# Lightning attention and a low-rank mixer: the masked quarter of the scores left out from step twelve, with the keys of every second pair of heads turned

## The chip, the cores and the metric

The kernel runs on one core of a Trainium2 chip. The metric is the time on the device of one execution, in microseconds (us), as the median of several runs. Before the change it is 673.5 us (three runs, 673.49 to 673.6).

## What is computed

Two blocks, one after the other, in float32. The first is linear attention with a decay per head, for 4 batches, 8 heads, 768 rows and 64 elements a head:

```python
Dmask = np.where(rel >= 0, lam ** rel, 0.0)            # rel = query row - key row
intra = einsum('bhic,bhjc->bhij', qb, kb) * Dmask      # scores, masked
intra = einsum('bhij,bhjd->bhid', intra, vb)
inter = einsum('bhid,bhde->bhie', qb * lam_pow, kv_state)
out   = intra + inter
kv_state = lam_block * kv_state + einsum('bhsd,bhse->bhde', kb * rev_pow, vb)
```

What matters here: a score counts only where the query row is not before the key row. In a tile of 128 keys by 128 queries, the quarter with the keys 64 to 127 and the queries 0 to 63 is zero after the mask. (The reference works in blocks of 64 rows, the kernel in tiles of 128; the result is the same.)

The second block mixes along the sequence with rank 32, `u = x + (U V)-mix of x`, and ends with `u + max(u @ w_ch1, 0) @ w_ch2`, where w_ch1 is 512 x 2048. These two products are most of the time.

## The kernel before, in words

The attention stage takes 24 steps, `s = 0..23`: a step is one tile of 128 rows of one batch, all 8 heads (6 tiles a batch, so step 12 is the first of the third batch). Heads go in four pairs, `a = 0..3`, with `x = 0, 1` inside a pair. Each step has these pieces; the order on every engine is the order in which the program is written, as the stage is put under a manual schedule (the list `pieces`, lines 553 to 574):

- `prep(s+1)`: q and k of the next step are transposed on TensorE (L348, banks pq and pk), and ScalarE copies them to qt and kt (L351).
- `scale(s+1)`: GpSimd multiplies qt by powers of the decay (qs, L376) and the k of the step after (ks, L365).
- `mix(s-7)` (pu L506 on TensorE, x_nat L509 on VectorE), and at the first step of a batch also `low` (pp L461) and `low_rows` (p_h L481, later the low part L487 on VectorE; ScalarE copies h, h2 and l2, L492, L493, L496, which the next `mix` reads). pp lies in the bank tag of pq.
- `intra(s)`: masked scores times v (px L446), after which ScalarE copies px to x_nat (L451).
- `state(s)`: the new state of keys and values (pkv L411, in the bank tag of pk; kv L417 or L419 on VectorE). Left out in a batch's last step.
- `turned`: ScalarE's u_hl (L542) and GpSimd's u_d (L543) for an earlier tile.
- `scores(s+1)` (pss L393), `inter(s+1)` (px L434), `masked(s+1)` (L402, VectorE), `fade(s+1)` (faded L385, ScalarE).
- `turn(s-7)`: the mixed tile is transposed (put L523), VectorE takes its high and low parts (ut L528, u_hl L539).
- Between them pieces of the preparation of the weights (`aside` and `late`: sc, m, wf, w on VectorE and ScalarE, L154 to L217).

One matmul in float32 is two records in the trace. Scores are written with the keys on the partitions of pss and the queries along its columns. In steps 0 to 11 a score matmul covers 128 keys; from step 12 on it is cut in two halves of 64 keys, so that each matmul uses a quarter of the array (`x` chooses the rows, the half of the keys the columns). sm, the masked scores, is one buffer; pss is one buffer of two banks, x in the first and the second.

From 121 us on come the two large products (`hidden`, L722 and L732, and `product`, L855 to L859).

Of the kernel before, what the change touches and what calls it, by code (L numbers as in the profile page):

```python
# [8 lines left out]
FP32 = mybir.dt.float32  # L9
# [3 lines left out]
ALU = mybir.AluOpType  # L13

P = 128
# [3 lines left out]
def kernel(  # L19
# [28 lines left out]
    nc = tc.nc  # L48

    B, H, S, D = q.shape  # L50
    HP = H // 2
    NT = S // P
# [45 lines left out]
    def tmp(name):  # L98
        return wconv.tile([P, C], FP32, tag="tmp", bufs=3, name=name)
# [139 lines left out]
    att = att_ctx.enter_context(tc.tile_pool(name="att", bufs=1))  # L239
# [5 lines left out]
    def two_banks(name, tag):  # L245
        return psf.tile([P, 2, N], FP32, tag=tag, name=name)
# [12 lines left out]
    raw = {}  # L259
# [30 lines left out]
    mask = consts.tile([P, 2, HP, P], FP32, name="mask")  # L290
# [33 lines left out]

    xs = {}
    st = {}
    kv = {}
    half = [slice(0, D), slice(D, P)]  # L330
# [55 lines left out]

    def scores(s):
        qt, kt = st[s]["qt"], st[s]["kt"]
        st[s]["pss"] = pss = two_banks("pss", "pss").rearrange("p x (a i) -> p x a i", a=HP)
        for a in range(HP):  # L390
            for x in range(2):
                for rows in half if s >= 2 * NT else [slice(0, P)]:
                    nc.tensor.matmul(  # L393
                        out=pss[rows, x, a, :], lhsT=kt[half[x], a, rows],
                        rhs=qt[half[x], a, :], start=True, stop=True,
                    )

    def masked(s):
        pss = st[s].pop("pss")
        st[s]["sm"] = sm = att.tile([P, 2, HP, P], FP32, tag="sm", bufs=1, name="sm")  # L400
        for x in range(2):
            nc.vector.tensor_tensor(out=sm[:, x], in0=pss[:, x], in1=mask[:, x], op=ALU.mult)  # L402

    def state(s):
        c = s % NT
# [33 lines left out]
    def intra(s):  # L439
        first = s % NT == 0  # L440
        sm, vr, px = st[s]["sm"], raw[s, "v"], st[s]["px"]
        px = px[:, :, 0 : HP * D].rearrange("p x (a e) -> p x a e", a=HP)
        for a in range(HP):
            for x in range(2):
                for t in range(2):
                    nc.tensor.matmul(  # L446
                        out=px[half[t], x, a, :], lhsT=sm[:, x, a, half[t]],
                        rhs=vr[:, 2 * a + x, :], start=(first and a == 0), stop=(a == HP - 1),
                    )
        xs[s] = x_pool.tile([P, C], FP32, tag="x", name="x_nat")  # L450
        nc.scalar.copy(xs[s].rearrange("p (a x e) -> p x a e", a=HP, x=2), px)  # L451


    pps = {}
# [56 lines left out]
    uhl, ud, turned = {}, {}, {}  # L511
# [42 lines left out]
    for s in range(NS):  # L554
        b, c = divmod(s, NT)
        done = s - NT - 1
        more = s + 1 < NS
        step = [("prep", s + 1), ("scale", s + 1)] * more
        step += [("late", s - 1)] * (s == NT)
        step += [("mix", done)] * (0 <= done < NS - NT - 1)  # L560
        step += [("low", b - 1)] * (c == 0 and b > 0)
        step += [("low_rows", b - 1)] * (c == 0 and b > 0)
        step += [("intra", s)]
        step += [("next_of_low", b - 1)] * (c == 0 and b > 0)
        step += [("late", s)] * (s < NT - 1 or s == NT) + [("state", s)]
        step += [("next_of_low", b - 1)] * (c == 0 and b > 0)
        step += [("turned", done - 1)] * (done > 0) + [("late", s)] * (done >= 0)
        step += [("next_of_low", b - 1)] * (c == 0 and b > 0)
        step += [("scores", s + 1)] * more
        step += [("aside", s)] * (s >= 2 * NT)  # L570
        step += [("inter", s + 1), ("masked", s + 1), ("fade", s + 1)] * more
        step += [("aside", s)] * (s < 2 * NT)
        step += [("turn", done)] * (done >= 0 and done // TG < FG)
        pieces += step
    waiting = {name: list(range(NS)) for name in "qkv"}

    def load_next(name, engine=nc.sync):
# [3 lines left out]

    run = {
        "prep": prep, "fade": fade, "scores": scores, "masked": masked, "inter": inter,
        "intra": intra, "state": state,
        "low": low, "low_rows": low_rows, "next_of_low": next_of_low, "mix": mix, "turn": turn,
        "scale": scale, "turned": lambda s: turned.pop(s)(),
    }
    def v_steps():

# [186 lines left out]
    c0, b = NS - NT, B - 1  # L776
# [181 lines left out]
```

## Time and profile before

| | |
|---|---|
| time, median of 3 | 673.5 us |
| span of the profiled execution | 672.5 us |
| attention stage | 0 to about 121 us, 24 steps |
| TensorE busy, 60 to 80, 80 to 100, 100 to 120 us | 19.54, 19.93, 19.68 of 20 us |
| VectorE busy in the same stretches | 19.51, 18.49, 18.44 |
| ScalarE busy in the same stretches | 13.51, 12.40, 14.23 |
| GpSimd busy in the same stretches | 12.56, 13.23, 14.61 |
| granted TensorE clock | 1.00 throughout |

Busy time of TensorE is from modelled ends of pipelined matmuls, so that a busy engine isn't yet one at its peak; the distance from the start of one group to that of the next tells what a group holds of the engine. An idle engine matters only where another waits for it. The view that tells this is the chain that ended last: the last instruction, what released it, what released that, and so on back to the start. For each piece it gives the start, the length and the engine, tile and line. Where the name of the engine changes, TensorE waited.

### The profile page before, as it was taken

Reading aid. Unit: us, or ns where it says so; the run is one execution under the profiler, and the core shown is the slowest. Engines: PE = TensorE matmul, PEld = TensorE weight load, DVE = VectorE, ACT = ScalarE, POOL = GpSimd, SP = SyncE. Lnnn points to the kernel's source line nnn. Section 1 sums busy time; section 2 is a strip of 40 time slices with the busy share of each in tenths; the row PEclk is TensorE's granted clock in tenths of the full one; section 3 lists DMA queues with packets and bytes.
Section 4 is the critical chain, followed back from the end, with each engine's and each line's share of the span. In section 5 each row is a group of like instructions: output and inputs, shape, how many; then the busy total and the mean of one; then the engine's idle time right before and its main releaser. Section 6 shows DMA issues by size and latency. Waiting matters only on the chain.

```text
span 672.5 us, 13170 instructions
## 1 busy us (share of the span) xinstructions
PE 665.9 (99%) x5124; PEld 545.4 (81%) x5124; DVE 496.6 (74%) x873; ACT 278.7 (41%) x517; POOL 112.8 (17%) x92
## 2 busy tenths in 40 slices
PE   9999999999999999999999999999999999999997
PEld 8888898787888888888888888888888888888885
DVE  4679999777999777777797255786586775865854
ACT  4675767454555444444455121332232322322320
POOL 4455667340000000000000000030030200300300
PEclk9999999999999999999999999999999999999999
DMA  9999993264776555555587999854363363443421
GB/s 208 214 228 239 237 232 109 84 215 156 235 276 240 204 203 204 204 203 204 203 280 253 325 314 387 291 185 140 94 206 107 110 204 94 158 155 95 161 89 62
DMA packets 131775, 131.27 MB, mean 195 GB/s; under 512 B 81346, under 2 KB 89794, under 8 KB 131714
## 3 DMA queue, kind: packets, MB, share of 16 engines
q1 hardware_dynamic: 130656, 130.18, 61.3%
q8 instruction: 40, 0.66, 0.4%
q10 hardware_dynamic: 1058, 0.26, 0.2%
q14 instruction: 21, 0.17, 0.1%
HBM read 80.09 MB, written 50.33 MB: 194 GB/s over the span
## 4 chain that ended last, share of the span: by engine, by line
PE 96%; DVE 2%; ACT 2%; issue 0%; DVEq 0%; ACTq 0%
PE pz L722 27%; PE pz L857 13%; PE pd L732 13%; PE pz L855 13%; PE pd L859 13%; PE pss L393 3%; PE px L446 3%; PE put L523 2%; PE pq L348 2%; PE px L434 1%; PE pkv L411 1%; PE pk L348 1%; PE pp L461 1%; PE pu L506 1%; PE idle L336 0%; ACT qt L351 0%
## 5 line engine op out<-in xcount | busy, mean ns | idle before, releaser
L722 PE MATMUL pz<-u_hl,w 128*128 128x512 f32 x768 | 190.4, 397 | 0.0
L722 PEld LDWEIGHTS pz<-u_hl,w 128*128 128x128 f32 x768 | 144.0, 188 | 35.5 <-issue 0.4
L857 PE MATMUL pz<-w_hl,m 128*128 128x512 f32 x384 | 151.1, 396 | 0.0
L855 PE MATMUL pz<-w_hl,m 128*128 128x512 f32 x384 | 150.9, 396 | 0.0
L859 PE MATMUL pd<-w_d,m 128*128 128x512 f32 x384 | 149.5, 396 | 0.0
L838 ACT ACTIVATE m<-mt 128x512 fp32r<-128x512 f32 x96 | 60.7, 633 | 196.0 <-PE pd L859 141.7
L839 DVE SCALAR_TENSOR_TENSOR m<-rm,m 128x512 fp32r<-128x512 f32 x96 | 71.4, 745 | 52.2 <-ACT m L838 52.1
L884 POOL TENSOR_TENSOR o<-o,u 128x512 f32<-128x512 f32 x20 | 29.9, 1529 | 447.3 <-DVE o L880 447.3
L737 DVE SCALAR_TENSOR_TENSOR r<-pd,r 128x512 f32<-128x512 f32 x96 | 61.8, 685 | 54.0 <-ACT r L728 43.5
L732 PE MATMUL pd<-u_d,w 128*128 128x512 f32 x384 | 98.6, 397 | 0.0
L728 ACT ACTIVATE r<-pz 128x512 f32<-128x512 f32 x96 | 52.2, 596 | 93.6 <-PE pz L722 92.9
L857 PEld LDWEIGHTS pz<-w_hl,m 128*128 128x128 f32 x384 | 72.3, 188 | 17.7
L855 PEld LDWEIGHTS pz<-w_hl,m 128*128 128x128 f32 x384 | 72.3, 188 | 17.6
L859 PEld LDWEIGHTS pd<-w_d,m 128*128 128x128 f32 x384 | 72.3, 188 | 17.6
L732 PEld LDWEIGHTS pd<-u_d,w 128*128 128x128 f32 x384 | 72.1, 188 | 17.3
L840 DVE SCALAR_TENSOR_TENSOR m<-m 128x512 fp32r<-128x512 f32 x96 | 69.0, 720 | 0.9
L837 DVE TENSOR_SCALAR mt<-rm 128x512 uint32<-128x512 uint32 x96 | 46.1, 481 | 28.0 <-DMA rm<-r_d 27.6
L402 DVE TENSOR_TENSOR sm<-pss,mask 128x512 f32<-128x512 f32 x48 | 30.8, 683 | 7.4 <-PE pss L393 7.3
L205 ACT CAST w<-wt 128x512 fp32r<-128x512 f32 x32 | 19.9, 622 | 30.5 <-DVE wt L202 23.4
L376 POOL TENSOR_TENSOR qs<-qt,powq 128x512 f32<-128x512 f32 x20 | 25.9, 1296 | 23.3 <-ACT qt L351 22.3
L446 PEld LDWEIGHTS px<-vraw,sm 128*64 128x64 f32 x768 | 24.7, 137 | 6.0 <-issue 2.4
L446 PE MATMUL px<-vraw,sm 128*64 128x64 f32 x768 | 28.3, 226 | 0.5 <-DVE sm L402 0.4
(88 smaller groups left out, 682.7 us busy)
## 6 DMA issues: line engine op xcount, KB each, us to landing
r_d<-r SPq DMA_DIRECT2D x96, 256.0 KB, 2.5
rm<-r_d SPq DMA_DIRECT2D x96, 256.0 KB, 2.7
words<-in_moe_w_ch_dram SPq DMA_DIRECT2D x30, 512.0 KB, 4.4
w_d<-w SPq DMA_DIRECT2D x16, 768.0 KB, 3.3
w_hl<-w_d SPq DMA_DIRECT2D x16, 512.0 KB, 6.2
vraw<-in_v_dram SPq DMA_DIRECT2D x24, 256.0 KB, 4.6
u_d<-x_nat SPq DMA_DIRECT2D x24, 256.0 KB, 3.5
u<-u_d SPq DMA_DIRECT2D x24, 256.0 KB, 4.1
```

Source lines behind the costliest of these rows:

```text
L446: nc.tensor.matmul(out=px[half[t], x, a, :], lhsT=sm[:, x, a, half[t]], rhs=vr[:, 2 * a + x, :], start=(first and a == 0), stop=(a == HP - 1),
L722: nc.tensor.matmul(out=acc[g][0], lhsT=w[:, n, ct, :], rhs=uhl[g][:, n, ct, :], start=(ct == 0 and n == 0), stop=(ct == CT - 1 and n == 1),)
L728: nc.scalar.mul(rs[g], acc[g][0], 4096.0 + 1.0)
L732: nc.tensor.matmul(out=acc[g][1], lhsT=w[:, 2, ct, :], rhs=ud[g][:, ct, :], start=(ct == 0), stop=(ct == CT - 1),)
L737: nc.vector.scalar_tensor_tensor(rs[g], acc[g][1], 4096.0, rs[g], ALU.mult, ALU.add)
L837: nc.vector.tensor_scalar(t.bitcast(U32), r.bitcast(U32), HI, None, ALU.bitwise_and)
L838: nc.scalar.activation(out=m[:, 0], in_=t, func=AF.Relu)
L839: nc.vector.scalar_tensor_tensor(m[:, 1], r, 0.0, hi, ALU.max, ALU.subtract)
L840: nc.vector.scalar_tensor_tensor(m[:, 2], hi, E, low, ALU.mult, ALU.subtract)
L855: nc.tensor.matmul(out=pz, lhsT=m[:, 0, cols], rhs=hl[:, 0], start=first, stop=False)
L857: nc.tensor.matmul(out=pz, lhsT=m[:, 1, cols], rhs=hl[:, 1], start=False, stop=end)
L859: nc.tensor.matmul(out=pd, lhsT=m[:, 2, cols], rhs=dd, start=first, stop=end)
```

## The change

From step 12 on (`TURNED = 2 * NT`), the matmul for the second half of the keys streams only the 64 queries that it can have a score with; the masked quarter isn't computed. In pairs a = 1 and 3 the halves of the keys are exchanged: keys 64 to 127 go to partitions 0 to 63 of pss and keys 0 to 63 to the others. So each quarter of the array gets two matmuls of 128 columns and two of 64 in a step. In the quarter that isn't written, pss still holds finite numbers of step 11, which the mask sets to zero; for this, pss becomes one tile that is allocated once.

The exchange has to be followed by whatever meets those scores: the mask of the odd pairs is turned by ScalarE over a scratch tile, in three copies in steps 9, 10 and 11 (`turn_mask`), and v of the odd heads' pairs is turned for each step by two ScalarE copies of 64 x 256 into vs (`turn_v`), which stand in ScalarE's queue just after x_nat's copy of the step before. Apart from that, the mask becomes one VectorE operation of 128 x 1024 in every step in place of two of 128 x 512.

```diff
+    sums = two_banks("pss", "pss")
+    TURNED = 2 * NT
...
     def scores(s):
         qt, kt = st[s]["qt"], st[s]["kt"]
-        st[s]["pss"] = pss = two_banks("pss", "pss").rearrange("p x (a i) -> p x a i", a=HP)
+        st[s]["pss"] = pss = sums.rearrange("p x (a i) -> p x a i", a=HP)
         for a in range(HP):
             for x in range(2):
-                for rows in half if s >= 2 * NT else [slice(0, P)]:
+                for o in range(2) if s >= TURNED else ():
+                    i = o if a % 2 == 0 else 1 - o
+                    cols = slice(i * D, P)
                     nc.tensor.matmul(
-                        out=pss[rows, x, a, :], lhsT=kt[half[x], a, rows],
+                        out=pss[half[o], x, a, cols], lhsT=kt[half[x], a, half[i]],
+                        rhs=qt[half[x], a, cols], start=True, stop=True,
+                    )
+                if s < TURNED:
+                    nc.tensor.matmul(
+                        out=pss[:, x, a, :], lhsT=kt[half[x], a, :],
                         rhs=qt[half[x], a, :], start=True, stop=True,
                     )
...
-        for x in range(2):
-            nc.vector.tensor_tensor(out=sm[:, x], in0=pss[:, x], in1=mask[:, x], op=ALU.mult)
+        nc.vector.tensor_tensor(out=sm, in0=pss, in1=mask, op=ALU.mult)
...
-                        rhs=vr[:, 2 * a + x, :], start=(first and a == 0), stop=(a == HP - 1),
+                        rhs=vs[s][:, a // 2, x, :] if s >= TURNED and a % 2 else vr[:, 2 * a + x, :],
+                        start=(first and a == 0), stop=(a == HP - 1),
...
+    def turn_v(s):
+        odd = raw[s, "v"].rearrange("p (j b x) d -> p j b x d", b=2, x=2)[:, :, 1]
+        vs[s] = att.tile([P, HP // 2, 2, D], FP32, tag="vs", name="vs")
+        for i in range(2):
+            nc.scalar.copy(vs[s][half[1 - i]], odd[half[i]])
+
+    odd_mask = mask[:, :, 1::2, :]
+
+    def turn_mask(n):
+        if n == 0:
+            held.append(tmp("turned").rearrange("p (x j i) -> p x j i", x=2, j=HP // 2))
+        if n < 2:
+            nc.scalar.copy(held[0][half[1 - n]], odd_mask[half[n]])
+        else:
+            nc.scalar.copy(odd_mask, held.pop())
...
-        step += [("intra", s)]
+        step += [("intra", s)] + [("turn_v", s + 1)] * (more and s + 1 >= TURNED)
+        step += [("turn_mask", s - TURNED + 3)] * (TURNED - 3 <= s < TURNED)
```

More of the change, by code (lines that the diff above doesn't have):

```diff
@@ L319 @@
     r_pool = None
+    sums = two_banks("pss", "pss")
+    TURNED = 2 * NT
     xs = {}
+    vs, held = {}, []
     st = {}
@@ L451, in intra @@
         nc.scalar.copy(xs[s].rearrange("p (a x e) -> p x a e", a=HP, x=2), px)
+        vs.pop(s, None)
+    def turn_v(s):
[11 more added lines that the diff above has]
+            nc.scalar.copy(odd_mask, held.pop())
     pps = {}
@@ L585 @@
         "low": low, "low_rows": low_rows, "next_of_low": next_of_low, "mix": mix, "turn": turn,
-        "scale": scale, "turned": lambda s: turned.pop(s)(),
+        "turn_v": turn_v, "turn_mask": turn_mask, "scale": scale, "turned": lambda s: turned.pop(s)(),
     }
```

## The prediction

> **What bounds the kernel now.** I read the page first: the busy times, the chain that ended last and the group of the mask.
>
> ```profile
> PE 665.9 (99%) x5124; PEld 545.4 (81%) x5124; DVE 496.6 (74%) x873; ACT 278.7 (41%) x517; POOL 112.8 (17%) x92
> ...
> PE 96%; DVE 2%; ACT 2%; issue 0%; DVEq 0%; ACTq 0%
> ...
> L402 DVE TENSOR_TENSOR sm<-pss,mask 128x512 f32<-128x512 f32 x48 | 30.8, 683 | 7.4 <-PE pss L393 7.3
> ```
>
> TensorE carries the span, with some 2% each on VectorE and ScalarE. The change lies in the attention stage alone (0 to 121 us; from 120 on the windows show PE busy 20.00 of 20.00, so what that stage gains or loses reaches the end). So I asked where inside it the chain leaves TensorE. First, what a step's scores cost, in the timeline of PE (start, length, engine, line, tiles, count):
>
> ```profile
> 78.78 1.10 PE L393 MATMUL pss<-qt,kt 64*64 64x128 f32 x32
> 79.71 0.64 PE L434 MATMUL px<-kv,qs 64*64 64x64 f32 x32
> 80.28 0.66 PE L523 MATMUL put<-ident,x_nat 128*128 128x128 f32 x4
> ```
>
> Both groups are 32 records (16 matmuls, two each) on four 64x64 quarters of the array, 8 records a quarter. With 128 columns the group holds TensorE 79.71 - 78.78 = 0.93 us, with 64 columns 80.28 - 79.71 = 0.57. Thus 8 records of half the width save 0.36 us, 4 save 0.18.
>
> Then the chain of waits, in order of time, around steps 11 to 13 and 18 to 19:
>
> ```profile
> 60.57 1.28 DVE sc L179
> ...
> 63.83 0.66 PE put L523 x4
> ...
> 65.01 0.60 ACT qt L351
> ...
> 65.65 1.52 PE pp L461 x48
> 67.17 1.11 PE px L446 x32
> ...
> 68.30 0.59 ACT x_nat L451
> 68.88 0.53 ACT vp L492
> ...
> 72.90 0.49 ACT kt L351
> ...
> 73.43 0.69 PE pkv L411 x16
> ```
>
> ```profile
> 98.50 0.43 DVE kv L417
> ...
> 100.95 1.30 DVE sm L402 x2
> ...
> 102.29 1.03 PE px L446 x28
> ```
>
> Here the chain goes over ScalarE without a break from the copy of x (step 12, 68.30) to the copy of kt (ends 73.38), for which the state product waits (pkv shares kt's bank). In step 18 it goes over VectorE, but the timeline shows ScalarE just as full beside it, and the state product on its heels:
>
> ```profile
> 102.51 0.58 ACT L351 COPY kt<-pk 128x512 f32<-128x512 f32 x1
> 103.16 0.67 PE L411 MATMUL pkv<-vraw,ks 128*64 128x64 f32 x16
> 35.41 1.03 ACT L612 CAST vp<-vt 32x384 fp32r<-32x384 f32 x2
> ```
>
> (The last line is the nearest price for a copy between two places in SBUF: 0.52 us for 384 elements.)
>
> **The Trainium skill.** "TensorE: Matmul & The Clock Gate", Part 3, says that small tiles' matmuls run concurrently; 32 records of 269 ns (the row of pss) inside 1.10 us agree. It also says that matmuls are strictly first in, first out at start and end; with equal widths this trace can't show whether a short one waits for a long one in another quarter. "TensorEngine Tiling (Array Packing)", Key Properties, says tiles operate independently. The first page (Architectural detail) says ACT and DVE are strict FIFO; the run of ACT operations above, in program order with no gap, agrees. "VectorE: DVE Perf Modes", on the TRN2 errata, prices a ScalarE SBUF copy at (224 + elements) cycles of 1.2 GHz: 0.51 us for 384, as measured (1.03 for two).
>
> **The change, part by part.**
> 1. *Masked quarter left out*, 12 steps. Each quarter of the array takes 4 records of 128 and 4 of 64 columns where it took 8 of 128: 0.18 us a step if the quarters run independently (the odd pairs are turned just so that each gets the same sum), 12 x 0.18 = 2.2 us at most; 0 if a group of four goes at its longest member's pace. I take 0.18.
> 2. *Mask in one operation*, 24 steps. Two cost 1.29 us. From 256 elements (kv, 0.42) to 512 (0.68) is 0.26, so 1,024 take 0.68 + 0.52 = 1.20: 0.09 us less of VectorE a step. intra needs both halves after its first four records, so this is gain only where the mask is on the chain: about 0.1 at step 11.
> 3. *turn_v*, 12 times two ScalarE copies of 64x256 behind x_nat's. Bounds: 0.27 (the 32x128 copies, 1.07 for four) and 0.52 each. The skill's formula gives (224 + 256)/1.2 = 0.40, an estimate; so 0.80 us a step. Queued behind: u_hl, the spreads of the low-rank rows, faded, then qt and kt of the next step, for which scores, pkv and GpSimd's qs wait. In an ordinary step it is hidden: after faded ends (80.51) ScalarE idles 0.96 us until pq, and kt (ends 82.54) is done 0.4 before pkv (82.95). In steps 12 and 18 there is no idle: the 0.80 goes whole to kt and pkv. At 18, kt goes from 103.09 to 103.89, pkv to 103.94 instead of 103.16: +0.78.
> 4. *turn_mask*, steps 9 to 11, 0.62 us each (as the 512-element casts). At step 9 ScalarE is full from 52.77 to 57.17 (exponents); kt ends 57.17 + 0.60 and pkv starts at 57.81 instead of 57.50: +0.31. At step 10 it idles 2.1 us: nothing. At step 11 both turns stand ahead of u_hl and qt: x_nat 62.98 (0.31 late), turns to 64.26, mask copy to 64.88, u_hl to 65.5, qt then instead of 65.01, so pp starts near 66.1 instead of 65.65: +0.45, which takes in the 0.31. The masked product of step 12 now waits for the mask copy (64.93 instead of 63.73, VectorE 1.1 late); behind it on VectorE stand wf, ut, u_hl, x_nat, p_h, kv, low part, wt, mask 13. That puts intra 13 at about 73.35; but ScalarE's own lateness, 0.45 + 0.80, puts pkv 13 at 74.68, and intra ends by 74.3. So it hides behind part 3.
> 5. *One pss tile for all steps, vs instead of v in odd pairs, vs's buffer*: nothing. The bank was single before and intra waits for the same mask; the copies for step s + 1 end some 2 us before intra s + 1; they reuse a buffer whose readers x_nat's copy has already waited for. v of a step lands about 4 us ahead of turn_v (issue near 54.3 for step 12, landing median 4.6).
>
> **Sum.** At pkv 13: +0.45 + 0.80 = +1.25. The scores of 12 and 13 gain nothing, as VectorE (put at 63.83 waits for x_nat) and ScalarE set the pace there. Scores 14 to 18 gain 5 x 0.18 = 0.90: +0.35. Step 18: +0.78, and scores 19 lost: +1.13. Scores 20 to 23 gain 0.72: +0.41. Two small waits come back: in step 20 a cast stands with the turns before faded and kt (about 0.2 at pkv 21), and in step 23 mask and intra have no transposes between them (0.1). Together +0.7, less 0.1 for the mask: **+0.6 us, 674.1 us**.
>
> **Rivals.**
> - *A, all of the saving arrives*: ScalarE is 41% busy, and if its copies are cheap (0.27 us) or run on past each other as 64-element faded do (1.06 for four), steps 12 and 18 lose little: 673.5 - 2.2 = 671.3 us. Against it: the unbroken ScalarE chain; even at 0.27 each, steps 12 and 18 cost 0.54 each.
> - *B, the quarters go in step*: a short matmul waits for the long one beside it; no saving, while +1.25 and +0.78 stay: 675.5 us, slower. For it: the skill's sentence on strict order. Against it: the Tiling page's sentence on independent tiles, and the even sums, by which a quarter that runs ahead is never more than one matmul ahead.
> - *C, VectorE takes over*: it is busy 19.51 of 20 us in 60 to 80 and 18.4 later, so a shorter TensorE step uncovers it. Step 16 on has 0.5 us between mask and intra, and the mask gives 0.09 a step; worth 0.3 to 0.5 more, 674.5 us.
>
> **How the numbers follow.** Forecast 0.38, C 0.12, A 0.24, B 0.26. The forecast's own spread (copies 0.27 to 0.52 in two places: -0.5 to +0.5; score saving 0.14 to 0.20) is 673.3 to 674.9. Faster by over 0.2% means under 672.15: most of A, 0.23. Slower means over 674.85: nearly all of B and a little of the forecast, 0.29. The rest, 0.48, is no change. Range 671.6 to 675.6, from A's better part to B.
>
> **What would show it.** Right: scores of a later step take 0.75 us from their start to inter's; mask one operation near 1.2 us; ScalarE without idle from x_nat 12 to kt 14, pkv 13 released by kt, about 1.2 us later than 73.43; pkv 19 released by kt; the step 14 to 17 distance 4.55 us instead of 4.73. Wrong: scores still at 0.9 us (B), pkv 13 and 19 as early as before (A), or intra waiting for sm in steps 14 to 17 (C).

## The result, and the profile after

The changed kernel takes 677.3 us (median of six runs, 675.3 to 678.4) beside 674.0 us for the kernel before in the same set (six runs). The ratio is 1.0039, with an interval of [1.0021, 1.0057]: slower by about 2.6 us by the ratio (the two medians are 3.3 us apart), where +0.6 us had been forecast. The time lies outside the forecast's range, 671.6 to 675.6 us. Run once more it was 1.0034 [1.0022, 1.0047].

The page of the kernel after, the three lines that answer to those of before (busy times, the chain by engine, the group of the mask):

```profile
PE 664.4 (99%) x5124; PEld 543.6 (81%) x5124; DVE 495.8 (74%) x849; ACT 289.9 (43%) x544; POOL 111.1 (16%) x92
...
PE 94%; ACT 3%; DVE 2%; issue 0%; DVEq 0%; ACTq 0%
...
L411 DVE TENSOR_TENSOR sm<-pss,mask 128x1024 f32<-128x1024 f32 x24 | 29.3, 1222 | 8.7 <-PE pss L403 6.4
```

TensorE is busy 1.5 us less, so the change did take work away. ScalarE is busy 11.2 us more (24 copies of v, three of the mask), and its share of the chain of waits rises from 2% to 3% while TensorE's falls from 96% to 94%. TensorE's work became shorter, and it waits longer: from 50 to 126 us its idle time that other engines ended grows from 0.6 us in all to 3.7. (A change of the engine's name in the chain says only who released the next piece last. TensorE need not have stood idle meanwhile: before, it shows no idle time ahead of pkv at 73.43, where the chain comes back to it from ScalarE.)

Next a step's scores, in the timeline of TensorE (start, length, engine, line, operation, tiles, shapes, count). Before, it was 0.93 us from the scores' start to inter's, and 0.57 us from there to the next group:

```profile
80.32 0.90 PE L398 MATMUL pss<-qt,kt 64*64 64x128 f32 x32
81.08 0.69 PE L443 MATMUL px<-kv,qs 64*64 64x64 f32 x32
81.71 0.66 PE L550 MATMUL put<-ident,x_nat 128*128 128x128 f32 x4
```

The scores hold TensorE for 81.08 - 80.32 = 0.76 us. But inter, which is unchanged, now holds it for 81.71 - 81.08 = 0.63.

The chain of waits, first around steps 11 to 13, then in step 18:

```profile
63.46 0.41 ACT vs L468
63.88 0.41 ACT vs L468
64.31 0.63 ACT mask L478
64.96 1.23 DVE sm L411
66.19 1.18 DVE wf L184
...
70.46 0.44 DVE kv L426
...
72.65 1.24 DVE sm L411
...
73.93 1.15 PE px L455 x32
```

```profile
99.09 0.60 ACT x_nat L461
99.70 0.40 ACT vs L468
100.11 0.40 ACT vs L468
...
100.54 0.62 ACT vp L519
...
104.63 0.49 ACT kt L354
...
105.16 0.69 PE pkv L420 x16
```

In the first, the copy of the mask (64.31) releases step 12's masked product, and from there the chain runs on VectorE for nearly nine microseconds, over a piece of the weights (wf), kv and the masked product of step 13, to intra of step 13 at 73.93 (71.83 before). In the second, the copies of v stand between x_nat and the casts of the low-rank rows, ScalarE has no idle time before kt, and the state product of step 19 starts at 105.16 instead of 103.16. The same place before, on ScalarE, for comparison:

```profile
98.03 0.59 ACT L451 COPY x_nat<-px 128x512 f32<-128x512 f32 x1 [2.21 <-PE px L446]
98.51 0.61 ACT L492 CAST vp<-p_h 32x512 fp32r<-32x512 f32 x1
```

To see where the time went I cut the attention stage at the starts of intra: "9 to 12" is the distance from intra of step 9 to intra of step 12. All values are in us and come from the profiled executions. The kernel after and its second run agree in every column from step 9 on within 0.05, so these columns carry the comparison. The stretch from the start to step 9 varies with the loads (see below). From the first large product to the end every kernel here took 550.7 to 551.3. Each row is a single execution.

| difference to before, us | 9 to 12 | 12 to 14 | 14 to 17 | 17 to 18 | 18 to 20 | 20 to first product | sum from 9 |
|---|---|---|---|---|---|---|---|
| before (length) | 15.53 | 10.13 | 14.21 | 5.39 | 10.12 | 14.50 | 69.88 |
| after | +0.66 | +1.22 | -0.35 | -0.14 | +0.84 | -0.18 | +2.05 |
| cut_only | 0 | -0.12 | -0.34 | -0.20 | -0.06 | -0.38 | -1.10 |
| turned_full | +0.67 | +1.33 | -0.01 | 0 | +0.96 | +0.15 | +3.10 |
| one_mask | +0.67 (store) | +0.21 (store) | 0 | 0 | +0.01 | +0.06 | +0.95 |
| no_turn_v | +1.62 (store) | +0.83 | +0.21 | -0.20 | -0.07 | -0.38 | +2.01 |
| no_turn_mask | 0 | +0.83 | -0.35 | +0.07 | +0.84 | -0.17 | +1.22 |
| before_copies | +0.75 (store) | +0.95 | 0 | +0.28 | +0.95 | +0.10 | +3.03 |
| after_store | +0.66 | +1.22 | -0.35 | -0.14 | +0.84 | -0.17 | +2.06 |
| turn_by_pool | -0.23 | +0.76 (store) | +1.28 (store) | -0.21 | +0.06 | -0.18 | +1.48 |
| turn_by_pool_store | -0.23 | +1.29 (v) | -0.35 | -0.21 | +0.06 | -0.18 | +0.38 |

"(store)" and "(v)" mark a stretch in which an engine waited for a transfer: ScalarE's copy of px to x_nat for the store of the tile that had its buffer before, or a copy of v for v. The 2.05 us of the changed kernel lie inside both intervals of the times (1.4 to 3.8 us and 1.5 to 3.2 us).

### The profile page after: what moved, and what is told of

Its sections match the earlier page's. It is cut to its first block, busy times and chain, and to the rows that moved or that the text cites. A ratio compares the mean times of both kernels' runs of the same rounds, so it can differ in the third digit from the quotient of the medians.

```text
span 674.0 us, 13174 instructions
## 1 busy us (share of the span) xinstructions
PE 664.4 (99%) x5124; PEld 543.6 (81%) x5124; DVE 495.8 (74%) x849; ACT 289.9 (43%) x544; POOL 111.1 (16%) x92
## 4 chain that ended last, share of the span: by engine, by line
PE 94%; ACT 3%; DVE 2%; issue 0%; DVEq 0%; ACTq 0%
PE pz L750 27%; PE pz L885 13%; PE pz L883 13%; PE pd L760 13%; PE pd L887 13%; PE px L455 3%; PE pss L403 2%; PE put L550 1%; PE px L443 1%; PE pq L351 1%; PE pkv L420 1%; PE pk L351 1%; PE pss L398 1%; PE pp L488 1%; PE pu L533 1%; DVE sm L411 1%
## 5 line engine op out<-in xcount | busy, mean ns | idle before, releaser
L411 DVE TENSOR_TENSOR sm<-pss,mask 128x1024 f32<-128x1024 f32 x24 | 29.3, 1222 | 8.7 <-PE pss L403 6.4
L455 PE MATMUL px<-vraw,sm 128*64 128x64 f32 x576 | 24.1, 226 | 0.6 <-DVE sm L411 0.4
L455 PEld LDWEIGHTS px<-vraw,sm 128*64 128x64 f32 x576 | 19.8, 137 | 6.0 <-DVE sm L411 2.4
```

What stands on the lines that cost most here:

```text
L455: nc.tensor.matmul(out=px[half[t], x, a, :], lhsT=sm[:, x, a, half[t]], rhs=vs[s][:, a // 2, x, :] if s >= TURNED and a % 2 else vr[:, 2 * ...
```

## The experiments

All comparisons are with the kernel before in the same set of runs, and the ratios are given with 95% intervals. My theory after the result: ScalarE's copies are the loss, in the stretches where ScalarE has no idle time, and the saving in the scores is real but smaller. In the expectations this is theory 1. Rivals: the saving doesn't arrive at all (theory 2); the single mask operation costs (theory 3); the transfers are what got slower (theory T in the later ones).

### The change again, and its parts by leaving out

**after_again** is the changed kernel, unedited.

> The changed kernel once more, beside the parts below. In its trace the attention stage ends 1.7 us later than before (first pz at 123.17 instead of 121.45 us), so all theories expect +1.5 to +2.6 us. If the ratio comes out near 1.0025, the rest of the +0.39% measured was scatter between runs; if it stays at 1.004, something outside the profiled execution's chain costs another us.

Measured: 1.0034 [1.0022, 1.0047]. The loss repeats, in the same stretches.

**cut_only** leaves both kinds of copies out:

```diff
-  rhs=vs[s][:, a // 2, x, :] if s >= TURNED and a % 2 else vr[:, 2 * a + x, :],
+  rhs=vr[:, 2 * a + x, :],
...
-  step += [("intra", s)] + [("turn_v", s + 1)] * (more and s + 1 >= TURNED)
-  step += [("turn_mask", s - TURNED + 3)] * (TURNED - 3 <= s < TURNED)
+  step += [("intra", s)]
```

> The cut scores and the single mask, without any turning on ScalarE (turn_v and turn_mask left out; the odd pairs' scores then meet an unturned mask and an unturned v, so that part of the output isn't the reference's). Theory 1, ScalarE's copies are the whole loss: a step from 14 on takes 4.62 us instead of 4.73, so 12 steps give about -1.1 to -1.3 us, ratio 0.998 to 0.9985. Theory 2, quarters of the array out of step with each other or scores beside inter cost time: no gain, +0 us or more. Theory 3, the single mask holds intra up: +0.5 us or more.

Measured: 0.9985 [0.9976, 0.9995], some 1.0 us faster. So the saving arrives: 0.34 us in the three steps from 14 to 17, 0.11 a step. In its timeline the scores hold TensorE for 0.76 us and inter for 0.62, as in the changed kernel; in turned_full, which turns everything but streams all 128 columns, inter holds it for 0.58. So inter's extra 0.05 belongs to the shorter scores and not to the turning.

**turned_full** does everything that the change does, but streams all 128 columns:

```diff
-  cols = slice(i * D, P)
+  cols = slice(0, P)
```

> The whole change, except that the score matmuls stream all 128 columns as before (keys of odd pairs still turned, all ScalarE copies still there). Theory 1: the saving of 0.11 us a step goes and the copies stay, so 1.0 to 1.2 us above the changed kernel, about +2.7 to +3.5 us against before. Theory 2: the uneven matmuls were the loss, so at or below the changed kernel.

Measured: 1.0056 [1.0042, 1.0069], some 3.8 us slower (2.8 to 4.7). The stretch from 14 to 17 is back at its old length, and the losses in 12 to 14 and 18 to 20 stay. It is the copies without the gain.

**one_mask** is the kernel before with the mask in one operation:

```diff
-  for x in range(2):
-      nc.vector.tensor_tensor(out=sm[:, x], in0=pss[:, x], in1=mask[:, x], op=ALU.mult)
+  nc.vector.tensor_tensor(out=sm, in0=pss, in1=mask, op=ALU.mult)
```

> The kernel before with the mask as one operation of 128 x 1024 and nothing else. Theories 1 and 2: within 0.3 us of before (VectorE saves 0.06 to 0.09 us a step, intra waits 0.05 us more where it had begun on the first half). Theory 3: +0.5 us or more, with intra's waits for sm longer than the 2.0 us in all of before.

Measured: 1.0000 [0.9991, 1.0009]. In the time the mask operation is neither gain nor loss. In the trace the stretch from 9 to 12 is 0.67 longer, as x_nat's copy of step 10 waited 2.2 us for a store, and the start to step 9 is 0.92 shorter. Where no transfer intervenes, from 14 to 20, the trace is that of before to 0.01 us.

**no_turn_v** and **no_turn_mask** each leave one kind of copies out:

```diff
# no_turn_v
-  rhs=vs[s][:, a // 2, x, :] if s >= TURNED and a % 2 else vr[:, 2 * a + x, :],
+  rhs=vr[:, 2 * a + x, :],
...
-  step += [("intra", s)] + [("turn_v", s + 1)] * (more and s + 1 >= TURNED)
+  step += [("intra", s)]
...
# no_turn_mask
-  step += [("turn_mask", s - TURNED + 3)] * (TURNED - 3 <= s < TURNED)
```

> The changed kernel with the mask turned but v not (the odd pairs' masked scores then meet an unturned v, so that part of the output isn't the reference's). Theory 1, ScalarE's full stretches: the mask's copies cost by their own some 0.2 us at step 9 and 0.4 to 0.6 us at steps 11 to 13, the cut gives 1.1 to 1.3 back, so -0.4 to -0.8 us against before; pkv of step 19 no longer waits 0.6 us for kt. Rival, the single wait of the masked product of step 12 for the mask copy is most of the loss: +0.5 us or more.

> The changed kernel with v turned but the mask not (the odd pairs' scores then meet an unturned mask, so that part of the output isn't the reference's). Theory 1: the turns of v in steps 12 and 18 cost about 1 us each, the cut gives 1.1 to 1.3, so +0.5 to +1.0 us against before, 0.6 to 0.9 below the changed kernel. Rival, the mask copies are most of the loss: below before.

Measured: 1.0006 [0.9994, 1.0018] without the copies of v, 1.0015 [1.0004, 1.0025] without those of the mask, where the change as a whole is 1.0034 to 1.0039. Both kinds cost. no_turn_mask came as theory 1 said. no_turn_v came with neither: theory 1 had it 0.4 to 0.8 us faster than before, the rival at least 0.5 us slower, and it is 0.4 us slower, with an interval from 0.4 us faster to 1.2 us slower.

In the trace of no_turn_mask the stretch 9 to 12 is as before (+0 instead of +0.66) and 12 to 14 is at +0.83 instead of +1.22: in these two stretches the mask's three copies cost 0.66 + 0.39 = 1.05 us. (From step 9 to the first product the two differ by 0.83 only, as no_turn_mask is 0.21 longer than the changed kernel from 17 to 18, long after the mask's copies; why is open.) In no_turn_v the loss in 18 to 20 is gone (-0.07). Its stretch 9 to 12 can't be read for the mask, as x_nat's copy of step 9 began late and the state product of step 10 then waited 1.05 us for kt. The profile puts the copy's idle time down to a score matmul, which the copy doesn't read. More likely it was a store: the copy began at 54.69, and the store issued at 49.48 took 5.1 us to land, to 54.58. In one_mask the store that the copy is shown to wait for landed as close ahead of it, at 58.35 for 58.46.

Of note in 12 to 14: the mask's copies alone (no_turn_v) make it 0.83 longer, those of v alone (no_turn_mask) also 0.83, so 0.95 each against cut_only, and both together 1.34. They hide behind each other in part, and neither hides wholly.

### The copies of v by themselves, and elsewhere

**before_copies** puts the twelve pairs of copies into the kernel before, where the change has them. Nothing reads them, and scores and mask stay as they were:

```diff
...
-  step += [("intra", s)]
+  step += [("intra", s)] + [("turn_v", s + 1)] * (more and s + 1 >= 2 * NT)
...
```

> The kernel before with the 12 pairs of copies of v alone, on ScalarE in the places that the change gives them; nothing reads them, scores and mask stay as before. Theory 1 (the copies cost what they take out of ScalarE's full stretches, whatever the scores do): 12 to 14 some 0.8 longer, 18 to 20 some 0.9 longer, 14 to 17 as before, the first product 1.7 to 2.2 us later than before, time +1.7 to +2.2 us (ratio 1.0025 to 1.0033). Rival (they cost only because the shorter scores leave ScalarE less time, and because the masked product waits for them): +0.3 us or less.

Measured: 1.0033 [1.0021, 1.0045], 2.2 us. The two longest of TensorE's waits on ScalarE in its trace (engine, line, releaser, us in total, times, longest):

```profile
PE pkv L411 <- ACT kt L351: 1.5, 4, 0.5
PE pu L514 <- ACT vp L504: 1.3, 2, 0.7
```

By stretches: 0.95 + 0.28 + 0.95 + 0.10 = 2.28 us from step 12 on. (The 0.75 in 9 to 12 is another matter: there x_nat's copies waited 1.4, 0.6 and 1.2 us for a store.) The copies of v cost about the same, 2.28 us here and 2.1 in the change, whether or not the scores are cut and whether or not anybody reads them: the time is ScalarE's, as theory 1 has it.

**turn_ahead** makes the same copies up to two steps ahead, in two buffers, and none in steps 12 and 18:

```diff
-  vs[s] = att.tile([P, HP // 2, 2, D], FP32, tag="vs", name="vs")
+  vs[s] = att.tile([P, HP // 2, 2, D], FP32, tag="vs", bufs=2, name="vs")
...
+  ahead_of = {10: (12,), 11: (13,), 13: (14,), 14: (15, 16), 15: (17,), 16: (18,), 17: (19,)}
+  ahead_of.update({s: (s + 1,) for s in range(19, NS - 1)})
...
-  step += [("intra", s)] + [("turn_v", s + 1)] * (more and s + 1 >= TURNED)
+  step += [("intra", s)] + [("turn_v", n) for n in ahead_of.get(s, ())]
```

> The changed kernel with the same copies of v, but vs in two buffers and the copies up to two steps ahead, so that none stands in steps 12 and 18 (two in step 14). The same work on ScalarE and the same output. Theory 1, it is where the copies stand: kt of step 18 and the state product of step 19 come about 1 us earlier than in the changed kernel, step 12's copies about 0.5 to 1 us earlier (VectorE's wait for the mask copy stays), so 1.3 to 1.8 us below the changed kernel, -0.3 to +0.3 against before. Rival, it is the amount of work on ScalarE that counts: within 0.4 us of the changed kernel.

Measured: 1.0044 [1.0028, 1.0061], no gain where theory 1 had one of 1.3 to 1.8 us over the changed kernel. The loss of step 18 went (18 to 20: -0.06), which agrees with theory 1, but a new one came. In the timeline of ScalarE (in brackets the idle time before, and what ended it):

```profile
62.93 0.82 ACT L468 COPY vs<-vraw 64x256 f32<-64x256 f32 x2 [2.47 <-DMA vraw<-in_v_dram]
```

v hadn't landed, and everything behind the copy waited with it, 4.8 us in two places (68.66 is the other); a copy of x also waited 2.4 us for a store. "v lands about 4 us ahead" holds for the change, whose copies stand a step later and show no such wait, but leaves no room for more.

**load_turned** has no copies on ScalarE. k and v of heads 4 to 7 are loaded with their halves exchanged, by three transfers in place of one for v, and VectorE makes a second mask and multiplies by the two in two operations (the transfers alone are shown):

```diff
+  for heads, rows, turn in ((slice(0, 4), slice(0, P), 0),
+                            (slice(4, 8), slice(0, D), D), (slice(4, 8), slice(D, P), -D)):
...
```

> The cut without copies on ScalarE: from step 12 on k and v are loaded with the halves of the heads 4 to 7 exchanged (three transfers in place of one), so that scores, masked product and state all meet the same order; these pairs take the place of the odd ones, a second mask and decay for them are built by VectorE in steps 1 to 6, the masked product is two operations from step 12 on. Theory 1: as the cut alone, -1.0 to -1.7 us against before. Rival, the transfers' queue becomes late (four more issues of 0.37 to 0.65 us a step in a queue that carries some 2.2 us of issues in a step of 4.7): loads of k or q late, +0.5 us or more.

Measured: 1.0228 [1.0209, 1.0246], some 15 us slower where theory 1 had it 1.0 to 1.7 us faster; the rival came, and larger than said. The wait of ScalarE that leads its list:

```profile
ACT x_nat L477 <- DMA u_d<-x_nat: 22.8, 8, 4.6
```

The copy of x waits for the store of the tile that had its buffer before, and the store stands in one queue with the loads, which have become more. Turning by transfers is dearer here than turning by copies; VectorE's extra operations weren't tried apart from them.

### The mask turned early: what transfers cost

**mask_early** gives the mask a third slot for the turned pairs, filled in steps 2 and 3. To make room, one small tile (lam_row) moves to scratch memory. **mask_early_pool_four** has GpSimd make the copies of v for steps 12, 13, 18 and 19 on top of it:

```diff
-    mask = consts.tile([P, 2, HP, P], FP32, name="mask")
+    mask = consts.tile([P, 4, 3, P], FP32, name="mask")
...
+        nc.scalar.copy(mask[half[1 - n], :, 2, :], mask[half[n], :, 1, :])
...
-        step += [("turn_mask", s - TURNED + 3)] * (TURNED - 3 <= s < TURNED)
+        step += [("turn_mask", s - 2)] * (2 <= s < 4)
...
-    lam_row = consts.tile([1, H + P], FP32, name="lam_row")
+    lam_row = tmp("lam_row")[0:1, 0 : H + P]
...
# mask_early_pool_four
-    nc.scalar.copy(vs[s][half[1 - i]], odd[half[i]])
+    (nc.gpsimd.tensor_copy if s % NT < 2 else nc.scalar.copy)(vs[s][half[1 - i]], odd[half[i]])
```

> The changed kernel, but the mask has a third slot in each half for the turned odd pairs, filled by one ScalarE copy in step 2 and one in step 3, and the three copies of steps 9 to 11 are gone. Same output. Theory 1 (two losses: the mask's copies in steps 9 to 11, and the copies of v in steps 12, 17 and 18): the stretch from step 9 to 12 is as long as before (15.5 us instead of 16.2), 12 to 14 some 0.8 over before, 18 to 20 some 0.85 over; the first product starts near 122.2 us in the profile instead of 123.2, and the time lies 0.9 to 1.0 us below the changed kernel's, about 1.0 to 1.5 above before. Rival (the mask's copies are hidden behind the copies of v, as the prediction said of the last of them): the time of the changed kernel within 0.4 us, and the 12 to 14 stretch still 1.2 over before.

> As mask_early, but in four of the twelve steps (v for steps 12, 13, 18 and 19, which are copied where ScalarE has no idle time) GpSimd makes the two copies of v. Same output. Theory 1 (it is ScalarE's time in these steps and nothing else that is lost): the stretches 12 to 14, 17 to 18 and 18 to 20 are as in the kernel with the cut alone (0.1 to 0.2 below before), the first product starts at 120.0 to 120.4 us, and the time is about 1.0 us below before, 0.998 to 0.999 of it: faster than both. Rival (GpSimd is as short of time there, and its u_d and qs come late, or it waits for v to land): the loss returns as waits for GpSimd, time at or above before. Second rival (the copies' cost is not where they stand but what they do to the memory or to later steps): the time of mask_early.

Measured: 1.0055 [1.0037, 1.0072] and 1.0039 [1.0027, 1.0051]; both expectations failed in the time. From step 12 on the trace of mask_early is as theory 1 said (+0.83, -0.35, -0.14, +0.83, -0.17), and in mask_early_pool_four the stretch from 17 to 20 loses nothing any more (-0.21 and +0.06); but from 12 to 17 it loses 1.27 and 0.51, where copies of x wait for stores. The time is lost there and ahead of step 12. In mask_early, one line of the transfers' queue and one of ScalarE:

```profile
50.73 0.96 SPq L546 DMA_DIRECT2D u_d<-x_nat  x1
```

```profile
56.77 0.59 ACT L461 COPY x_nat<-px 128x512 f32<-128x512 f32 x1 [3.26 <-DMA u_d<-x_nat]
```

A store that is issued at 50.73 is done only at 56.77, six microseconds later (the median from issue to landing is 4.1 in this trace), and until then x_nat can't be written and px not read out.

**mask_early_again** and **mask_early_pool_four_again** repeat the two. **mask_early_pool_four_store** and **before_store** issue the store just after the mix, ahead of the load of v:

```diff
         nc.vector.tensor_tensor(out=xs[s], in0=pu, in1=xs[s], op=ALU.add)
+        if s < NS - NT - 1:
+            nc.sync.dma_start(out=u_d[s], in_=xs[s])
...
-        nc.sync.dma_start(out=u_d[s], in_=xs.pop(s))
+        if s >= NS - NT - 1:
+            nc.sync.dma_start(out=u_d[s], in_=xs[s])
+        xs.pop(s)
```

> The kernel of mask_early once more. In its trace the copy of x waited 3.3 us for the store of the tile that had its buffer before, and transfers moved 189 to 224 GB/s in the first 60 us, where the kernel before shows 198 to 250. Theory T (its time of 1.0055 came from transfers that were slow in that set of runs, and nothing in the kernel asks for it): this time without that wait, the first product near 122.2 us, the time 0.9 to 1.5 us above before (ratio 1.0013 to 1.0022), below the changed kernel's. Rival K (the early mask itself, its larger tile or its copies in steps 2 and 3, delays the transfers): 1.005 again, with the wait for the store again.

> The kernel of mask_early_pool_four once more. There steps 17 to 19 lost nothing any more, but six copies of x waited 7.6 us in all for stores. Theory T (slow transfers in that set of runs): first product at 120.0 to 121.0 us, time 0.3 to 1.0 us below before (ratio 0.9985 to 0.9995), so faster than both kernels. Rival K (a step that GpSimd helps along asks for transfers faster than they can be had, or GpSimd's wait for v holds the rest up): 1.002 or more again, with waits of the copy of x for stores.

> As mask_early_pool_four, and the store of the mixed tile (u_d from x_nat) is issued just after the mix, ahead of the loads of v and of the weights' words in the queue of transfers, and not after the transposes. Same output. If what is left of the loss is the copy of x that waits for a store which stands behind loads (theory T, the part that is the queue's order): no wait for stores, first product 120.0 to 120.6 us, ratio 0.9975 to 0.999. If the transfers are short as a whole (rival S), the loads of v come later by what the stores gain, and the wait moves to them: ratio as the run of mask_early_pool_four beside it, within 0.001.

> The kernel before with the same move of the store alone. Theory T: its profile shows no wait of the engines for stores to begin with, so its fastest runs stay where they are, and its median comes down by 0 to 0.8 us (ratio 0.9988 to 1.000), as the slower of its runs are those with waits for stores. Rival S (transfers short as a whole): 1.000 to 1.001.

Measured: 1.0050 [1.0034, 1.0066], 1.0026 [1.0015, 1.0038], 1.0003 [0.9991, 1.0015] and 0.9988 [0.9978, 0.9997]. The first two stay slow (theory T had them at 1.0013 to 1.0022 and 0.9985 to 0.9995), so that a passing slowness of the transfers isn't the reason, and theory T falls in that form. The early mask has a cost of its own: 1.0050 to 1.0055 where the changed kernel has 1.0034 to 1.0039, and with GpSimd's copies 1.0026 to 1.0039 where the next section has 0.9979 with the mask in its old place. The five traces with it start intra at 10.0 to 11.2 us (8.9 to 9.9 in the others) and reach step 9 later than before by 1.4 to 2.6 us, but the trace of no_turn_mask, which has no early mask, is 1.4 late there as well. What in the edit costs the time (the larger mask, its copies, the moved tile) is left open. The last two point to the wait for stores as a part of what GpSimd's version lost: with the store ahead of the loads no copy of x waits for one, and the ratio falls by 0.0023 from mask_early_pool_four_again, where before_store falls by 0.0012. With intervals of about 0.001 to either side on each ratio, the difference between the two isn't clear.

### The mask where it was, without ScalarE

**turn_by_pool** is the changed kernel with the mask's three copies made by GpSimd, and GpSimd's four pairs of copies of v as above. **turn_by_pool_store** adds the store's move, and **after_store** is the changed kernel with that move alone:

```diff
-    nc.scalar.copy(vs[s][half[1 - i]], odd[half[i]])
+    (nc.gpsimd.tensor_copy if s % NT < 2 else nc.scalar.copy)(vs[s][half[1 - i]], odd[half[i]])
...
-    nc.scalar.copy(held[0][half[1 - n]], odd_mask[half[n]])
+    nc.gpsimd.tensor_copy(held[0][half[1 - n]], odd_mask[half[n]])
...
-    nc.scalar.copy(odd_mask, held.pop())
+    nc.gpsimd.tensor_copy(odd_mask, held.pop())
```

> The changed kernel with the mask where it was (turned in steps 9 to 11), but GpSimd makes those three copies, and also the copies of v for steps 12, 13, 18 and 19; ScalarE makes the other eight pairs. Same output. Theory 1 (the loss is ScalarE's time in its full stretches and the chain behind the mask's copy): 9 to 12 as before (15.5 us), 12 to 14 at most 0.3 over before, 14 to 17 0.35 under, 17 to 20 as before or 0.2 under, first product at 120.2 to 120.9 us where the loads keep up; ratio 0.9985 to 1.000. Rival (as in mask_early_pool_four, the copies of x wait for stores): 1.002 to 1.004. If it stays well below mask_early_pool_four, the early mask had a cost of its own.

> As turn_by_pool, with the store of the mixed tile issued just after the mix, ahead of the load of v. Expected from the parts: the cut alone 0.9985, the store's move 0.9988 on the kernel before, both together 0.9973; with a little of the copies left (0.2 to 0.5 us) 0.9975 to 0.9985, so 672.5 to 673.3 us beside a before of 674.3: faster than both kernels. Rival (transfers short as a whole, so the gains overlap): 0.9985 to 1.000.

> The changed kernel with the move of the store alone. If part of its loss is the queue of transfers (copies of v and of x that wait), more is won here than on the kernel before (0.8 us): 1.2 to 1.6 us, ratio 1.0012 to 1.002. If its loss is the engines' alone, the store's move gives what it gave there: ratio 1.0022 to 1.003, with steps 12, 17 and 18 as long as in the changed kernel.

Measured: 0.9979 [0.9968, 0.9990], 0.9979 [0.9970, 0.9989] and 1.0017 [1.0006, 1.0028]. The first two compute the same as the changed kernel and are faster than both kernels, by some 1.4 us against before (0.0021 x 674) and 3.7 to 4.0 us against the change (0.0055 to 0.0060). Nothing was moved but ScalarE's work in the full stretches, to GpSimd. The clean comparison is turn_by_pool with before. turn_by_pool_store has the store's move besides, and against before_store it is 0.9979 / 0.9988 = 0.9991, which isn't clear of noise. Step 18 of turn_by_pool_store on ScalarE, and the state product of step 19 on TensorE:

```profile
97.35 0.58 ACT L461 COPY x_nat<-px 128x512 f32<-128x512 f32 x1 [2.21 <-PE px L455]
97.83 0.61 ACT L519 CAST vp<-p_h 32x512 fp32r<-32x512 f32 x1
...
101.82 0.58 ACT L354 COPY kt<-pk 128x512 f32<-128x512 f32 x1
```

```profile
102.65 0.64 PE L420 MATMUL pkv<-vraw,ks 128*64 128x64 f32 x16
```

The cast follows x_nat after 97.83 - 97.35 = 0.48 us, where the copies of v made it 1.45 (99.09 to 100.54), and the state product starts with no wait shown. So the loss of step 18 goes when the copies leave ScalarE's queue; turn_by_pool, without the store's move, has the same +0.06 in 18 to 20. GpSimd's copies are about as short as ScalarE's 0.41 (two groups of turn_by_pool: count, busy, mean ns, idle before):

```profile
L468 POOL COPY vs<-vraw 64x256 f32<-64x256 f32 x8 | 3.5, 441 | 0.6 <-POOL ks L368 0.2
L476 POOL COPY turned<-mask 64x512 f32<-64x512 f32 x2 | 1.2, 606 | 0.1
```

Not all is regained in the traces. In turn_by_pool_store the stretch 12 to 14 is 1.29 longer than before, with a wait of inter for GpSimd of 1.2 us; GpSimd's copy of v had once waited 1.0 us for v to land. In turn_by_pool x_nat's copies waited 2.9, 0.9 and 0.3 us for a store; its trace is of an execution of 674.9 us, where its times lie between 672.7 and 675.5.

after_store has the stretches of the changed kernel to 0.01 us, and none of its copies of x waits for a store, as none does in the changed kernel's trace. Its time decides less. The expectation put 1.0012 to 1.002 to the transfers' queue and 1.0022 to 1.003 to the engines; 1.0017 lies in the first, but its interval reaches into both. Against before_store it is 1.0017 / 0.9988 = 1.0029, 2.0 us, with an interval of about 1 us to either side as an estimate from the two. So the traces say that the changed kernel's loss is the engines', 2.05 us of it; that some tenths of a microsecond more are the queue's, in executions without a trace, is not excluded.

## Why the prediction was wrong

The likeliest case had the direction right, and most of the mechanism: copies on ScalarE, off the path in ordinary steps and on it in steps 12 and 18. Rival A (all of the saving, copies cheap) fell with cut_only, which gains 1.1 us and not 2.2 with no copies at all, and with before_copies, in which the copies cost 2.2. Rival B (no saving) fell with cut_only and turned_full. Rival C fell with TensorE's waits in the changed kernel's trace, none of which is intra waiting for sm in steps 14 to 17. What failed is the size of three terms, all in the same direction, and one overlap: the lateness of the masked product was said to hide behind ScalarE's, and it did not.

| term | forecast, us | shown, us |
|---|---|---|
| up to pkv or intra 13 (9 to 14) | +1.25 | +1.88 |
| scores 14 to 18 | -0.90 | -0.49 |
| step 18 | +0.78 | +0.84 |
| scores 20 to 23 and small waits | -0.42 | -0.18 |
| mask operation | -0.10 | 0 (one_mask) |
| sum | +0.6 | +2.05 |

- **Scores, 0.18 us a step.** The scores' own time was right (0.75 forecast, 0.76 found). What was mis-sized is that the group behind them gives a part back: inter 0.63 instead of 0.57. The distance from step to step falls from 4.73 to 4.62, not to 4.55. I took the distance to the next group's start for what a group costs; it should have been the distance over both. Nothing before could show by how much: there every group of the scores was full. cut_only gains 1.10 us from step 9 on where the forecast's two entries for the scores have 1.62. The sentence of the Trainium skill in "TensorEngine Tiling (Array Packing)", Key Properties, that tiles operate independently agrees with the 0.76 us; why inter is longer wasn't tried by itself.
- **turn_v, 0.40 us each.** The price of one was good: 0.41 us by the trace, 0.40 as estimated with the formula of the Trainium skill ("VectorE: DVE Perf Modes", on the TRN2 errata). But two of them cost 0.97 us of ScalarE's time and not 0.80. In step 18 the operation behind x_nat began 0.48 us after it before (98.03 to 98.51), while x_nat itself takes 0.59. With the copies it is 1.45: 0.61 from x_nat to the first, then 0.41 and 0.43. So the overlap of 0.11 behind x_nat is lost as well. That step 18 came out near (0.84 for 0.78) is in part luck: the state product of step 19 came 0.94 later, counted from intra 18, and 0.10 of it came back from the shorter scores behind it. Over steps 12 to 23 the copies of v cost 2.1 us in the change (after against cut_only, plus no_turn_mask in 12 to 14: 0.95 + 0.06 + 0.90 + 0.20) and 2.28 in before_copies, where the forecast has 0.80 + 0.78 + 0.2 = 1.78.
- **turn_mask, "+0.45, which takes in the 0.31" and "So it hides behind part 3".** This is the largest error: 1.05 us up to step 14, beside the copies of v, instead of 0.45. Three things went wrong. First the price, as with v: a copy of the mask was put at its own length, 0.62. In step 9, u_hl began 0.48 us after x_nat before (52.77 to 53.25) and 1.25 after it now (52.44 to 53.69), 0.77 more. So the state product of step 10, which waits for kt, came 0.47 later after intra (1.45 us instead of 0.98, from 56.52 to 57.50) where 0.31 was forecast:

```profile
56.19 1.15 PE L455 MATMUL px<-vraw,sm 128*64 128x64 f32 x32
57.64 0.69 PE L420 MATMUL pkv<-vraw,ks 128*64 128x64 f32 x16 [0.30 <-ACT kt L354]
```

The 0.30 of idle time isn't that delay: before, the state product started 0.17 us ahead of intra's modelled end (57.67), and this overlap is lost too.

Secondly, VectorE's chain from the masked product of step 12 to intra 13 was forecast at 8.42 us (64.93 to 73.35) and took 8.97 (64.96 to 73.93). VectorE doesn't wait in it; one piece, wf, grew by 0.50 us. The first two lines are of before, the last two of after (VectorE's and GpSimd's timelines):

```profile
64.93 0.77 DVE L184 SCALAR_TENSOR_TENSOR wf<-m,sc 128x512 f32<-128x512 f32 x1
63.87 1.29 POOL L543 TENSOR_TENSOR u_d<-u_hl 128x512 fp32r<-128x512 f32 x1 [2.57 <-ACT u_hl L542]
...
66.10 1.27 DVE L184 SCALAR_TENSOR_TENSOR wf<-m,sc 128x512 f32<-128x512 f32 x1
65.54 1.28 POOL L570 TENSOR_TENSOR u_d<-u_hl 128x512 fp32r<-128x512 f32 x1 [3.33 <-ACT u_hl L569]
```

wf ends 0.54 us after GpSimd's u_d in the first (65.70 and 65.16) and 0.55 in the second (67.37 and 66.82), whenever it began: it waited for u_d. And u_d was late because ScalarE's u_hl stood behind the copies of v and of the mask.

Thirdly, the two queues aren't apart. I had VectorE's lateness end before ScalarE's and so hide behind it. But ScalarE's casts of the low-rank rows need VectorE's p_h, and p_h was late:

```profile
70.46 0.62 ACT L519 CAST vp<-p_h 32x512 fp32r<-32x512 f32 x1 [0.41 <-DVE p_h L508]
```

Counted from intra 9, kt of step 13's state product ended 1.98 us later than before, and not 1.25: x_nat 0.66 late instead of 0.45, 0.92 for the copies of v instead of 0.80, and the 0.41 that the forecast hadn't. VectorE's chain came out level with it: intra 13, released by the masked product, ended at 75.08 and kt at 75.03, and the state product began at 75.09. A path that was called hidden with a margin of 0.4 us ended up on the chain of waits.

The signs that I had named for right and wrong: scores at 0.75 (came, 0.76), mask near 1.2 (1.22), pkv 19 released by kt (came, at +2.0 in all), step distance 4.55 (4.62), pkv 13 released by kt, 1.2 us late (came late, 75.09, but behind intra 13, which had waited 0.39 us for its masked product; in no_turn_mask, without the mask's copies, it does wait for kt, 0.46).

## What to carry to other kernels

Moving work from the busiest engine to a lightly used one is priced in the stretches in which the receiver has no idle time, and there it costs its full length and the overlap that it breaks, and its lateness goes on to the engines that wait for it and may come back from them (0.41 us here, from ScalarE over GpSimd and VectorE to ScalarE). Before putting new operations on an engine, look in the timeline for the stretch where another engine (here GpSimd, at the start of a batch) is idle, and put only those operations there: eleven of the 27 copies (four pairs of v, three of the mask) made by GpSimd turned +0.35% into -0.2%. And price a shortened group by the distance between steps, with the group behind it, and not by the distance to its neighbour's start.

## What the runs showed of the hardware that was not expected

- GpSimd copies 64 x 256 float32 in SBUF, from one half of the partitions to the other, in 0.44 us and 128 x 512 in 0.61, about as fast as ScalarE (0.41 and 0.62). Its two-operand operations of 128 x 512 take 1.1 to 1.3 us, or up to 1.8 where VectorE is in their way (next point).
- VectorE's wf (two operands in SBUF) and GpSimd's u_d and qs did not run side by side. In the thirteen traces in which wf begins well before u_d has ended, it ends 0.54 to 0.56 us after u_d, and so takes 0.76 to 1.47 us. In the others it takes 0.68, and where GpSimd's u_d or qs begins at the same time or while it runs, that one takes 1.57 to 1.82 instead of 1.28. Likewise VectorE's m took 1.53 us instead of 0.42 beside u_d in step 16 of no_turn_v (87.10 to 88.63, u_d 87.08 to 88.35), and intra 17 then waited 0.44 us for its masked product.
- With half of its matmuls at half width, the scores' group in quarters of the array holds TensorE for 0.76 us instead of 0.93, close to the 0.18 less that the groups of before gave (0.93 and 0.57). But the full group after it takes 0.05 to 0.06 us longer.
- In the attention stage the DMA engines are nearly always busy: 0.87 to 1.02 of their time in the stretches from 10 to 100 us of the kernels before and after, at 198 to 256 GB/s. A small change of order in the queue (the store ahead of a load) then lowered the ratio by 0.0012 (before), by 0.0017 to 0.0022 (the changed kernel) and by 0.0023 (mask_early_pool_four), the first hardly clear of noise, and by nothing in turn_by_pool. The distance from intra 0 to intra 9, in which most of these kernels do the same, was 41.5 to 43.9 us.
